# A decode kernel bound by its loads: softmax totals per pair of heads, three more folded value caches, other idle products, one value load cut 1 and 3

## The chip, the core and the metric

The kernel runs on one core of a Trainium2 chip, in one launch. A core has five engines that run apart from each other and meet at semaphores: TensorE (PE, matrix products; PEld is its weight load), VectorE (DVE), ScalarE (ACT), GpSimd (POOL) and SyncE (SP), which here only issues loads. Loads from HBM into on-chip memory (SBUF, 128 partitions) are carried out by 16 DMA engines. Products land in a second, small memory (PSUM). The metric is the device time of one execution in microseconds (us); lower is better.

## The reference

Two layers of attention for one new token over long key and value caches, each followed by a gated MLP, and each run twice with the same weights and caches:

```python
def _A_ref(x, k_cache, v_cache, wq, wo):
    B, Sq, D = x.shape
    H, Dh = 32, 128
    q = (lambda x, *d: x.transpose(*d))((x @ wq).reshape(B, Sq, H, Dh), 0, 2, 1, 3)
    scores = jnp.einsum("bhqd,bhkd->bhqk", q, k_cache) * (Dh ** -0.5)
    p = _softmax(scores, axis=-1)
    o = jnp.einsum("bhqk,bhkd->bhqd", p, v_cache)
    return (lambda x, *d: x.transpose(*d))(o, 0, 2, 1, 3).reshape(B, Sq, H * Dh) @ wo

x = x + _A_ref(_layernorm(x, axis=-1), A_k_cache, A_v_cache, A_wq, A_wo)
x = x + _B_ref(_layernorm(x, axis=-1), B_w_gate, B_w_up, B_w_down)
x = x + _A_ref(_layernorm(x, axis=-1), A_k_cache, A_v_cache, A_wq, A_wo)
x = x + _B_ref(_layernorm(x, axis=-1), B_w_gate, B_w_up, B_w_down)
```

B is 2, D is 576, the caches are [2, 32, 8192, 128] in float32 (268 MB each) and DF is 4608. Each attention reads both caches once, but for what the second finds still on chip from the first.

## The kernel before

**Items.** The caches are cut into 34 items, numbered 0 to 33. Items 0 to 29 (PAIRS is 30) are two neighbouring heads of one batch row: 8 MB of keys and 8 MB of values each, held as 128 partitions of 16384 numbers, 64 partitions a head. Even items are batch row 0 and odd ones row 1 of the same heads, so items 2j and 2j+1 belong together. Items 30 to 33 are single heads (SINGLE), 4 MB each. An item has 8 parts (4 for a single head) of 16 cache rows (PART, 2048 numbers a partition). Attention 0 goes through the items upwards, attention 1 downwards. Below, "keys 29" is the key cache of item 29.

**One item.** `multiply` forms key times query on DVE (line 744) in three stretches of 3, 3 and 2 parts; POOL adds the halves of each row (line 773); `add_up` sums the rest on DVE (line 776) and gives the stretch of SBUF free. Then `peak`, `highest` and `softmax` find the maximum and the weights, `total` (line 841) sums the weights over the partitions with a product with ones, `inverse` (line 847) takes the reciprocal on DVE, and `values` (line 909) multiplies weights and values on PE. An item's last `add_up` stands after the start of the next item; `values` of an item stands in the middle of the next item.

**Folding.** For items where `folds(n)` is true, the last two parts of the values are not multiplied on PE: `weigh` scales them on DVE (line 876), POOL adds them up in three halvings (line 879), and `folded` takes the short rest to PE (line 887). The `weigh` and `folded` of item n stand in item n+2. Until then the values stay in SBUF, whereas unfolded values are free once `values` has run in item n+1.

**Where loads go.** SBUF holds six slots of 4 MB (SLOT), and a ring of four small places for weights. A list of loads is written down once (`plan_first`, `plan_mlp`, `plan_second`); a small model (`Arena`) walks through the program, and a load is issued on SP in the list's order as soon as its place is free in that model. SP then waits at run time for the instructions that freed the place, and everything behind a waiting load in SP's queue waits too. An item of two heads takes two neighbouring slots, of (0,1), (2,3) and (4,5) the pair that has been free for longest:

```python
for s in sorted(range(0, NSLOT, 2), key=lambda s: max(self.freed[s:s + 2])):
    at = self.slots(key, (s, s + 1), 8)
```

At the end of attention 0 the slots are named in the plan instead (the tuple or the last number):

```python
k(SINGLE[0], (0,))
half(("v", 0, last), vc, last, 0, 1)
half(("v", 0, last), vc, last, 4, 5)
k(SINGLE[1], (3,))
v(SINGLE[0], (4,))
```

So keys 30 go to slot 0, the first half of values 29 (`last`) to slot 1, the second half to slot 5, keys 31 to slot 3.

**Between the attentions.** Weights pass through the ring in pieces of about 1 MB, 4 places, while PE multiplies them. `idle_products` puts products whose result nobody reads between the pieces. Attention 1 starts with keys 33 to 31, or parts of them, still in SBUF; the rest of its first caches is loaded part by part into places as they come free (`plan_second`), the values of item 30 into the place of values 33.

Of the kernel before, what the change touches and what calls it, by code (L numbers as in the profile page):

```python
# [9 lines left out]
F32 = mybir.dt.float32  # L10
# [5 lines left out]
P = 128  # L16
# [3 lines left out]
DH = 128  # L20
# [7 lines left out]
GH = 4  # L28
# [97 lines left out]
def decode_layers(ctx, tc, x_in, kc, vc, wq, wo, wg, wu, wd, out):  # L126
    nc = tc.nc
    scale = DH ** -0.5

    consts = ctx.enter_context(tc.tile_pool(name="consts", bufs=1))  # L130
    work = ctx.enter_context(tc.tile_pool(name="work", bufs=2))
# [8 lines left out]
    for c in range(4):  # L140
        for s in range(2):
            lo = 32 * c + s * B
# [66 lines left out]
    def several_parts(key, src, n, k, m, where, first):  # L209

        def make():
            at = places[where][first:first + m]
            if not all(arena.clear(a, PART) for a in at):
                return False
            for i, a in enumerate(at):
                arena.take((key, k + i), a, PART)
                ready.setdefault(key, {})[k + i] = part(a)
            load(at[0], n, src, k, k + m)
            return True

        queue.append(make)
# [169 lines left out]
    def plan_second():  # L391

        for k in range(4):
            of_half(1, k)
        half_rows(("wq", 1, NU - 1), wq, single[-1], None)
        for k in range(4):
            of_half(0, k)
        last = PAIRS - 1
        k63, v63, k62, v62 = ("k", 1, SINGLE[3]), ("v", 1, SINGLE[3]), ("k", 1, SINGLE[2]), ("v", 1, SINGLE[2])

        for k in range(2):
            by_rows(("k", 1, SINGLE[1]), kc, SINGLE[1], k, True)
        first, pair = ("k", 1, SINGLE[0]), ("k", 1, last)
        one(first, kc, SINGLE[0], 0, None)
        by_rows(("k", 1, SINGLE[1]), kc, SINGLE[1], 2, False)
        several_parts(first, kc, SINGLE[0], 1, 2, k63, 0)
        one(first, kc, SINGLE[0], 3, (k63, 2))
        one(pair, kc, last, 0, (k63, 3))
        for k in range(0, 4, 2):
            several_parts(("v", 1, SINGLE[0]), vc, SINGLE[0], k, 2, v63, k)  # L410
        for k, m, where, at in ((1, 2, k62, 0), (3, 2, k62, 2), (5, 2, v62, 0), (7, 1, v62, 2)):
            several_parts(pair, kc, last, k, m, where, at)
        half(("k", 1, last - 1), kc, last - 1, 0, 5)
        half(("k", 1, last - 1), kc, last - 1, 4, 4)
# [77 lines left out]
        )  # L492

    spread()
    home = consts.tile([P, 3 * DH + 20], F32, name="home")

# [18 lines left out]
    smalls = [bank2[:, 4 * GH + P + 2 * i:4 * GH + P + 2 * i + 2] for i in range(2)]  # L515
    low = bank2[:, 4 * GH + P + 4:]
    share = low[:, :FOLD * JC]
    kept = psum1.tile([P, JC, DH], F32, name="kept")

# [17 lines left out]
    def small(p, n):  # L537

        if n > 2:
            return turned[0:p, 0:n]  # L540
        smalls.append(smalls.pop(0))
        return smalls[0][0:p, 0:n]


    def norm(split=False, then=None):
# [62 lines left out]
    def attention(layer):  # L608
# [12 lines left out]
        def half_products(h):  # L621

            for k in range(4):
                key = ("wq", 1, h, k)
                q_products(
                    ready.pop(key).rearrange("p (c w) -> p c w", w=EQ), 64 * k + 8 + 4 * h, h,
                    k == 0, h == 0 and k == 3,
                )
                done(key)
                if k > 0 if h else k < 3:  # L630
                    idle_products(1)

        if layer == 0:
            for us in GU[0]:
# [202 lines left out]
                )  # L837

        def total(n):
            tot[n] = small(P, 2)  # L840
            nc.tensor.matmul(tot[n][:, :ITEMS[n].heads], ones, rs.pop(n), start=True, stop=True)  # L841

        def inverse(n):
            it, t = ITEMS[n], tot.pop(n)
            if it.heads == 2:
                rinv[n] = work.tile([P, 2], F32, name="rinv", bufs=4)
                nc.vector.reciprocal(rinv[n], t)
            else:
                if it.h not in of_head:
                    of_head[it.h] = work.tile([P, 2], F32, name="rinv", bufs=4)  # L850
                rinv[n] = of_head[it.h]
                nc.vector.reciprocal(rinv[n][:, it.b:it.b + 1], t[:, 0:1])

        of_head = {}

# [6 lines left out]

        def folds(n):

            return 3 <= n < PAIRS - 3

        def weigh(n):

# [65 lines left out]
        def divide(n, by_scalar=False):  # L934
            it = ITEMS[n]
            lo = 32 * (it.h % GH)
            if it.heads == 1:
                r = rinv[n]
                nc.vector.tensor_tensor(
                    out=oT[lo:lo + 32, it.h // GH, :, :, :],  # L940
                    in0=po[lo:lo + 32, :, :2].unsqueeze(2).to_broadcast([32, GH, 2, B]),
                    in1=r[lo:lo + 32, :].unsqueeze(1).unsqueeze(1).to_broadcast([32, GH, 2, B]),
                    op=ALU.mult,
                )
                return
            for b, i in ((b, i) for b in range(B) for i in range(2)):
                to = oT[lo + 32 * i:lo + 32 * i + 32, it.h // GH, :, :, b]
                o = po[lo:lo + 32, :, 2 * b + i:2 * b + i + 1].to_broadcast([32, GH, 2])
                ri = rinv[n - it.b + b][lo:lo + 32, i:i + 1]
                if by_scalar:  # L950
                    nc.scalar.activation(to, o, AF.Copy, scale=ri)
                else:
                    nc.vector.tensor_tensor(out=to, in0=o, in1=ri.unsqueeze(1).to_broadcast([32, GH, 2]), op=ALU.mult)
# [147 lines left out]
    def mlp(layer):  # L1101
# [10 lines left out]
        def split_products(h):  # L1112

            steps = [(("g", layer, h, u), u, 0) for u in range(4)] + [(("gu", layer, h), 4, 0)]
            steps += [(("u", layer, h, u), u, 1) for u in range(4)]
            for key, u, g in steps:
                w = ready.pop(key).rearrange("p (k c w) -> p k c w", c=4, w=HG)
                for k in range(2):
                    for c in range(4):
                        nc.tensor.matmul(  # L1120
                            acc[32 * c:32 * c + 4 * B, h, :HG], window(u, 4 * k + 2 * g), w[:, k, c, :],
                            start=(key == steps[0][0] and k == 0), stop=(key == steps[-1][0] and k == 1),
                        )
# [102 lines left out]
```

## Time and profile before

| | |
|---|---|
| median of three runs | 2683.0 us (2681.78 to 2683.21) |
| profiled execution: its own time | 2682.85 us |
| its span, first to last instruction | 2681.1 us |
| DVE busy | 1989.8 us (74%) |
| POOL busy | 1551.8 us (58%) |
| PE busy | 909.0 us (34%) |
| ACT busy | 165.4 us (6%) |
| load queue (q1) | 1152.40 MB, 99.8% of 16 engines' span |

Times in the rows are in us from the span's start, unless marked ns. A row of the order of time has start, duration, engine and line, operation, written<-read with shapes, a count, and in brackets how long the engine idled before it and what ended that. A row of stretches has the length, then busy time and count of PE, PEld, DVE, ACT and POOL, the granted PE clock (1 is full speed), the DMA engines' busy share and GB/s. SPq rows are loads being issued; what the load then takes is not in that row. A row of the chain has start, duration and what the chain ran through.

### The profile page before, as it was taken

To read this page: it belongs to the slowest core of one execution; us is meant where nothing else is said; L and a number is where in the kernel's file an instruction comes from. 1 tells how busy PE (TensorE), PEld (TensorE's weight loads), DVE (VectorE), ACT (ScalarE), POOL (GpSimd) and SP (SyncE) were. 2 spreads that over 40 slices of the span, in tenths; PEclk is the share of its full clock that TensorE was granted. 3 is DMA by queue.
4 is the path that set the end of the run, shared out by engine and by line. 5 is a ranking of instruction groups with operands and counts; after the bars stand their busy time and mean duration, and the time that the engine had idled before them with its cause. 6 is when DMAs were issued, how large, how long until landed. Compare 5 with 4: busy or idle time off the path is not lost.

```text
span 2681.1 us, 15549 instructions
## 1 busy us (share of the span) xinstructions
PE 909.0 (34%) x6276; PEld 284.4 (11%) x6276; DVE 1989.8 (74%) x935; ACT 165.4 (6%) x792; POOL 1551.8 (58%) x407
## 2 busy tenths in 40 slices
PE   1323332233223223334663333223222323332346
PEld 0100000000000000111221100000000000000022
DVE  4878888888788878867037778888888888888740
ACT  0000000000000000001026000000000000000000
POOL 2546676667666766744028457666766666676520
PEclk8656655665566566566986665566566556655678
DMA  9999999999999999999999999999999999999998
GB/s 423 438 430 431 435 434 431 434 432 434 434 432 433 434 432 435 429 430 428 416 411 430 436 429 433 434 434 432 430 436 434 431 434 433 434 432 432 435 428 383
DMA packets 29352, 1153.40 MB, mean 430 GB/s; under 512 B 3272, under 2 KB 3296, under 8 KB 4320
## 3 DMA queue, kind: packets, MB, share of 16 engines
q1 hardware_dynamic: 29240, 1152.40, 99.8%
q8 instruction: 49, 0.80, 0.1%
q14 instruction: 23, 0.19, 0.0%
q10 hardware_dynamic: 40, 0.01, 0.0%
HBM read 1152.39 MB, written 0.00 MB: 430 GB/s over the span
## 4 chain that ended last, share of the span: by engine, by line
DMA 67%; DVE 19%; PE 8%; ACT 3%; POOL 2%; issue 1%; SPq 0%; another core or an unknown queue 0%; POOLq 0%; ACTq 0%; DVEq 0%
DMA space<-in_A_k_cache_dram 57%; DVE space L744 17%; PE acc L887 3%; DMA space<-in_A_v_cache_dram 3%; DMA space<-in_B_w_down_dram 2%; POOL space L773 2%; ACT prz L833 2%; DVE scores L776 2%; PE bank L659 1%; DMA space<-in_B_w_up_dram 1%; DMA space<-in_B_w_gate_dram 1%; PE bank L841 1%; PE bank L810 1%; DMA space<-in_A_wo_dram 1%; ACT space L766 0%
## 5 line engine op out<-in xcount | busy, mean ns | idle before, releaser
L773 POOL TENSOR_TENSOR space<-space 128x3072 f32<-128x3072 f32 (+4 forms) x221 | 1128.0, 5104 | 476.3 <-DVE space L744 331.3
L744 DVE TENSOR_TENSOR space<-space,bank 128x6144 f32<-128x6144 f32 (+4 forms) x223 | 1111.8, 4986 | 343.6 <-DMA space<-in_A_k_cache_dram 270.9
L909 PE MATMUL acc<-space,prz 128*16 128x512 f32 (+1 forms) x3328 | 520.0, 790 | 346.4 <-DMA space<-in_A_v_cache_dram 342.3
L776 DVE TENSOR_REDUCE scores<-space 128x48 f32<-128x3072 f32 (+4 forms) x223 | 569.0, 2551 | 90.8 <-POOL space L773 90.6
L879 POOL TENSOR_TENSOR space<-space 128x2048 f32<-128x2048 f32 x144 | 389.8, 2707 | 384.0 <-DVE space L876 360.7
L659 PE MATMUL bank<-qsb,few 4*64 4x128 f32 (+1 forms) x256 | 46.2, 437 | 889.9 <-DVE space L744 881.9
L876 DVE TENSOR_TENSOR space<-space,bank 128x4096 f32<-128x4096 f32 x48 | 212.2, 4420 | 1.8 <-DVE bank L871 0.2
L909 PEld LDWEIGHTS acc<-space,prz 128*16 128x16 f32 (+1 forms) x3328 | 106.4, 118 | 742.0 <-DMA space<-in_A_v_cache_dram 378.7
L825 ACT ACTIVATE nbs<-bank 128x2 f32<-128x2 f32 (+1 forms) x68 | 11.6, 171 | 2010.2 <-PE bank L810 1973.1
L659 PEld LDWEIGHTS bank<-qsb,few 4*64 4x64 f32 (+1 forms) x256 | 20.8, 202 | 909.9 <-DVE space L744 892.0
L581 POOL TENSOR_TENSOR rstd<-ve,few 128x1 f32<-128x1 f32 x4 | 2.2, 550 | 177.0 <-DVE ve L579 177.0
L887 PE MATMUL acc<-space,few 128*16 128x512 f32 x96 | 90.6, 1047 | 0.0
L802 PE MATMUL bank<-ident,m 128*1 128x128 f32 x68 | 20.3, 298 | 196.3 <-DVE m L800 196.1
L1147 DVE STREAM_TRANSPOSE gu<-acc 128x288 f32<-128x288 f32 x4 | 1.9, 483 | 93.4 <-ACT acc L1145 93.4
L841 PE MATMUL bank<-few 128*128 128x2 f32 x120 | 35.3, 363 | 81.4 <-ACT prz L833 81.4
L932 PE MATMUL bank<-few,wide 128*32 128x4 f32 (+1 forms) x272 | 21.8, 203 | 119.3 <-DVE wide L924 119.3
L833 ACT ACTIVATE prz<-scores,nbs 64x128 f32<-64x128 f32 (+1 forms) x128 | 50.7, 396 | 11.7 <-POOL prz L823 8.8
L766 ACT ACTIVATE space<-space 128x128 f32<-128x128 f32 x164 | 48.4, 296 | 19.8 <-DVE space L744 16.7
L810 PE MATMUL bank<-m,few 1*128 1x2 f32 (+1 forms) x136 | 38.5, 350 | 27.4 <-DVE m L808 27.4
L585 DVE TENSOR_TENSOR x<-bank,x 128x144 f32<-128x144 f32 x4 | 1.2, 308 | 59.1 <-PE bank L1183 39.3
L923 DVE TENSOR_TENSOR acc<-acc,few 128x512 f32<-128x512 f32 x34 | 23.1, 680 | 29.2 <-PE acc L909 29.2
L760 POOL TENSOR_TENSOR space<-space,qs 128x512 f32<-128x512 f32 x23 | 29.2, 1272 | 19.7 <-ACT qs L741 19.7
(103 smaller groups left out, 524.2 us busy)
## 6 DMA issues: line engine op xcount, KB each, us to landing
space<-in_A_k_cache_dram SPq DMA_DIRECT2D x6, 4096.0 KB
space<-in_A_v_cache_dram SPq DMA_DIRECT2D x5, 4096.0 KB
space<-in_B_w_gate_dram SPq DMA_DIRECT2D x8, 1152.0 KB
space<-in_B_w_up_dram SPq DMA_DIRECT2D x8, 1152.0 KB
space<-in_B_w_down_dram SPq DMA_DIRECT2D x8, 1152.0 KB
space<-in_A_wq_dram SPq DMA_DIRECT2D x9, 1024.0 KB
space<-in_A_wo_dram SPq DMA_DIRECT2D x2, 4608.0 KB
space<-in_A_v_cache_dram SPq DMA_DIRECT2D x4, 2048.0 KB
```

What stands on the lines that cost most here:

```text
L659: nc.tensor.matmul(qb[n][to, :], pick[32 * c:32 * c + 4, r:r + 1].to_broadcast([4, P // it.heads]), qsb[32 * c:32 * c + 4, (h % 4) * DH:(h ...
L744: nc.vector.tensor_tensor(out=u[:, :r, :], in0=t[:, :r, :], in1=qb[n].unsqueeze(1).to_broadcast([P, r, DH]), op=ALU.mult)
L766: nc.scalar.activation(u[:, j, :], u[:, j, :], AF.Copy, accum_out=S[n][:, base(n, k) + j:base(n, k) + j + 1])
L773: nc.gpsimd.tensor_tensor(out=half, in0=half, in1=u[:, :r, DH // 2:], op=ALU.add)
L776: nc.vector.tensor_reduce(out=S[n][:, base(n, k):base(n, k) + own_rows(n, k, m)], in_=prod.pop((n, k)), axis=AX.X, op=ALU.add)
L810: nc.tensor.matmul(mT[n][:, :heads], ones[0:1, :], m1[:, :heads], start=True, stop=True)
L833: nc.scalar.activation(pr[at, lo:].rearrange("p (g e) -> p g e", e=4)[:, 0:it.rows // 2 * it.heads:2 * it.heads, :], s[at, :it.rows].rearr ...
L841: nc.tensor.matmul(tot[n][:, :ITEMS[n].heads], ones, rs.pop(n), start=True, stop=True)
L876: nc.vector.tensor_tensor(out=t, in0=t, in1=share.unsqueeze(2).to_broadcast([P, rows, DH]), op=ALU.mult)
L879: nc.gpsimd.tensor_tensor(out=t[:, :rows - less], in0=t[:, :rows - less], in1=t[:, less:rows], op=ALU.add)
L887: nc.tensor.matmul(accumulator(n)[0:16, :], owner[:, 8 * ITEMS[n].b:8 * ITEMS[n].b + 16], part_at(arena.live[key, lo][0], 4 * DH), start=F ...
L909: nc.tensor.matmul(accumulator(n)[32 * c:32 * c + m, :], pr[:, at:at + m], t[g // 4][:, g % 4 * 4:g % 4 * 4 + 4, :].rearrange("p j d -> p ...
```

## The change

1. `folds(n)` becomes `layer < n < PAIRS - 3` in place of `3 <= n < PAIRS - 3`: items 1 and 2 of attention 0 and item 2 of attention 1 are folded too.
2. `total` makes one product of 4 columns for two items that belong together, once the second is through, in place of one of 2 columns for each; `inverse` takes one reciprocal of 4 columns. The small PSUM places are given out anew for it, and `home` is 2 columns longer.
3. `idle_products`: between the query weights of attention 1, one product of 512 columns into the idle half of `acc` in place of two of 128 into another bank; between the second half of the first MLP's weights, mostly one of 256 columns into `acc` in place of two of 128.
4. Values 30 for attention 1 are loaded as 1 and 3 parts in place of 2 and 2, and parts 5 to 7 of keys 29 as 1 and 2 in place of 2 and 1.

```diff
-        for k in range(0, 4, 2):
-            several_parts(("v", 1, SINGLE[0]), vc, SINGLE[0], k, 2, v63, k)
-        for k, m, where, at in ((1, 2, k62, 0), (3, 2, k62, 2), (5, 2, v62, 0), (7, 1, v62, 2)):
+        for k, m in ((0, 1), (1, 3)):
+            several_parts(("v", 1, SINGLE[0]), vc, SINGLE[0], k, m, v63, k)
+        for k, m, where, at in ((1, 2, k62, 0), (3, 2, k62, 2), (5, 1, v62, 0), (6, 2, v62, 1)):
             several_parts(pair, kc, last, k, m, where, at)
...
                 if k > 0 if h else k < 3:
-                    idle_products(1)
+                    idle_products(2, 1 - h)
...
         def total(n):
-            tot[n] = small(P, 2)
-            nc.tensor.matmul(tot[n][:, :ITEMS[n].heads], ones, rs.pop(n), start=True, stop=True)
+
+            if ITEMS[n].heads == 1:
+                tot[n] = four[:, 0:1]
+                nc.tensor.matmul(tot[n], ones, rs.pop(n), start=True, stop=True)
+            elif completes(seq.index(n)):
+                tot[n] = four
+                nc.tensor.matmul(tot[n], ones, sums.rearrange("p a i -> p (a i)"), start=True, stop=True)
 
         def inverse(n):
-            it, t = ITEMS[n], tot.pop(n)
-            if it.heads == 2:
-                rinv[n] = work.tile([P, 2], F32, name="rinv", bufs=4)
+            it, t = ITEMS[n], tot.pop(n, None)
+            if it.heads == 2 and t is not None:
+                rinv[n] = work.tile([P, 4], F32, name="rinv", bufs=3)
                 nc.vector.reciprocal(rinv[n], t)
...
         def folds(n):
 
-            return 3 <= n < PAIRS - 3
+            return layer < n < PAIRS - 3
...
-                ri = rinv[n - it.b + b][lo:lo + 32, i:i + 1]
+                ri = rinv[n][lo:lo + 32, 2 * b + i:2 * b + i + 1]
...
                 if key != steps[-1][0]:
-                    idle_products(1, None if h else 1)
+                    idle_products(1, 1 - h if h == 0 or u else None)
```

How the order moves, at three places. In these rows `_49` is the part of a semaphore's name that all share. DMAHW0 to DMAHW7 count landings: the loads take the eight in turn, so a row that waits for DMAHW3 waits for the landing of one certain earlier load. DVE, PE, Activation and Pool are those engines' counts of done work.

First, SP's queue at the end of attention 0. The first two rows are keys 29 and values 28; keys 28, values 27, keys 29 and values 28 signal DMAHW1, 2, 3 and 4. The rows of 128x8192 are keys 30, the two halves of values 29, keys 31, values 30 and keys 32:

```order
 L168 DMA space<-in_A_k_cache_dram 128x16384 [waits DMAHW0_49,DVE_49,PE_49]
 L168 DMA space<-in_A_v_cache_dram 128x16384 [waits DMAHW2_49,PE_49]
-L168 DMA space<-in_A_k_cache_dram 128x8192 [waits DMAHW1_49,DVE_49]
+L168 DMA space<-in_A_k_cache_dram 128x8192 [waits DMAHW3_49,DVE_49]
 L168 DMA space<-in_A_v_cache_dram 128x8192 [waits DVE_49]
-L168 DMA space<-in_A_v_cache_dram 128x8192 [waits DMAHW4_49,PE_49]
-L168 DMA space<-in_A_k_cache_dram 128x8192 [waits DMAHW3_49,DVE_49]
+L168 DMA space<-in_A_v_cache_dram 128x8192 [waits DMAHW1_49]
+L168 DMA space<-in_A_k_cache_dram 128x8192 [waits DMAHW4_49,PE_49]
 L168 DMA space<-in_A_v_cache_dram 128x8192
 L168 DMA space<-in_A_k_cache_dram 128x8192
```

The order of the loads is the same, but slots 0 and 1, into which keys 30 and half of values 29 go, hold other caches by then. The three pairs of slots go round; as two more items are folded early on, each later cache stands two steps further round. Followed through `pair`, from the first loads on:

| cache | slots before | slots now |
|---|---|---|
| values 1, keys 4 | (4,5), (0,1) | (4,5), (4,5) |
| values 2, keys 5 | (4,5), (2,3) | (0,1), (0,1) |
| keys 28 | (0,1) | (4,5) |
| values 27 | (4,5) | (2,3) |
| keys 29 | (2,3) | (0,1) |
| values 28 | (4,5) | (2,3) |

Before, keys 30 wait until DVE is done with the first parts of keys 28; now they wait for the landing of keys 29 and until DVE is done with the first four parts of keys 29 (the sum over its second stretch).

Second, SP's queue at the start of attention 1, values 30 and then parts 1 to 7 of keys 29:

```order
 L168 DMA space<-in_A_k_cache_dram 128x4096
 L168 DMA space<-in_A_k_cache_dram 128x2048 x2
-L168 DMA space<-in_A_v_cache_dram 128x4096 x2
-L168 DMA space<-in_A_k_cache_dram 128x4096 x3
+L168 DMA space<-in_A_v_cache_dram 128x2048
+L168 DMA space<-in_A_v_cache_dram 128x6144
+L168 DMA space<-in_A_k_cache_dram 128x4096 x2
 L168 DMA space<-in_A_k_cache_dram 128x2048
+L168 DMA space<-in_A_k_cache_dram 128x4096
```

The first load of values 30 is one part and needs one part of the place free; the second needs the other three.

Third, PE at the same start, between the products with the query weights (line 616 before, 615 now), before:

```order
L616 MATMUL acc<-space,xt 4x512 x8
L592 MATMUL bank_124<-ident 4x128 x2
L616 MATMUL acc<-space,xt 4x512 x4
L592 MATMUL bank_124<-ident 4x128 x2
L616 MATMUL acc<-space,xt 4x512 x4
```

and now:

```order
L615 MATMUL acc<-space,xt 4x512 x8
L591 MATMUL acc<-ident 4x512
L615 MATMUL acc<-space,xt 4x512 x4
L591 MATMUL acc<-ident 4x512
L615 MATMUL acc<-space,xt 4x512 x4
```

The idle product is twice as many columns in one, and goes to the half of `acc` that the products beside it do not write.

More of the change, by code (lines that the diff above doesn't have):

```diff
@@ L494, in decode_layers @@
     spread()
-    home = consts.tile([P, 3 * DH + 20], F32, name="home")
+    home = consts.tile([P, 3 * DH + 22], F32, name="home")
     xt = consts.tile([P, PAD + NU * 32], F32, name="xt")
@@ L514, in decode_layers @@
     turned = bank2[:, 4 * GH:4 * GH + P]
-    smalls = [bank2[:, 4 * GH + P + 2 * i:4 * GH + P + 2 * i + 2] for i in range(2)]
-    low = bank2[:, 4 * GH + P + 4:]
+    pair, four = bank2[:, 4 * GH + P:4 * GH + P + 2], bank2[:, 4 * GH + P + 2:4 * GH + P + 6]
+    low = bank2[:, 4 * GH + P + 6:]
     share = low[:, :FOLD * JC]
@@ L540, in small @@
             return turned[0:p, 0:n]
-        smalls.append(smalls.pop(0))
-        return smalls[0][0:p, 0:n]
+        return pair[0:p, 0:n]
     def norm(split=False, then=None):
@@ L839, in total @@
         def total(n):
-            tot[n] = small(P, 2)
-            nc.tensor.matmul(tot[n][:, :ITEMS[n].heads], ones, rs.pop(n), start=True, stop=True)
+            if ITEMS[n].heads == 1:
[4 more added lines that the diff above has]
+                nc.tensor.matmul(tot[n], ones, sums.rearrange("p a i -> p (a i)"), start=True, stop=True)
         def inverse(n):
-            it, t = ITEMS[n], tot.pop(n)
-            if it.heads == 2:
-                rinv[n] = work.tile([P, 2], F32, name="rinv", bufs=4)
+            it, t = ITEMS[n], tot.pop(n, None)
+            if it.heads == 2 and t is not None:
+                rinv[n] = work.tile([P, 4], F32, name="rinv", bufs=3)
                 nc.vector.reciprocal(rinv[n], t)
-            else:
+            elif it.heads == 1:
                 if it.h not in of_head:
-                    of_head[it.h] = work.tile([P, 2], F32, name="rinv", bufs=4)
-                rinv[n] = of_head[it.h]
-                nc.vector.reciprocal(rinv[n][:, it.b:it.b + 1], t[:, 0:1])
+                    of_head[it.h] = work.tile([P, 4], F32, name="rinv", bufs=3)
+                rinv[n] = of_head[it.h][:, 0:2]
+                nc.vector.reciprocal(rinv[n][:, it.b:it.b + 1], t)
         of_head = {}
```

## The prediction

> **What bounds the kernel now.** I read the page's totals first, then stretches, then the order of time where the stretches stand out.
>
> ```profile
> span 2681.1 us, 15549 instructions
> DMA  9999999999999999999999999999999999999998
> GB/s 423 438 430 431 435 434 431 434 432 434 434 432 433 434 432 435 429 430 428 416 411 430 436 429 433 434 434 432 430 436 434 431 434 433 434 432 432 435 428 383
> q1 hardware_dynamic: 29240, 1152.40, 99.8%
> ```
>
> The load queue q1 has packets on the engines for 99.8% of the span, and the slices' GB/s row stays between 411 and 438 but for the last. A kernel whose loads never pause is as long as its bytes at that rate, plus whatever time the DMA engines stand still. So for each edit I ask one thing: does it add or remove a pause of the loads?
>
> ```profile
> 0.00:10.00 10.00, 0.00 (x0) 0.00 (x0) 4.41 (x29) 0.00 (x0) 0.70 (x6) 1.00 0.85 340
> 1160.00:1170.00 10.00, 0.66 (x9) 0.56 (x8) 9.96 (x6) 1.04 (x4) 9.30 (x2) 0.50 0.90 387
> 1400.00:1410.00 10.00, 5.55 (x34) 1.26 (x34) 8.98 (x8) 7.55 (x50) 9.36 (x8) 0.83 0.96 375
> 2670.00:2680.00 10.00, 6.32 (x148) 3.68 (x146) 0.31 (x1) 0.00 (x0) 0.00 (x0) 1.00 0.46 184
> ```
>
> In these stretches the last two numbers are the DMA share and GB/s. Pauses before are few: some 2 us at the start (340 of 433 GB/s), the last microseconds, when all has landed, and 10 x (1 - 375/433) = 1.3 us at 1400. The 387 at 1160 is an effect of where 10 us are cut, as packets are counted whole: the 67 us slice it lies in (the 18th) runs at 430. Nothing in this kernel can then win more than a few us, and a gap of 5.4 us (0.2% of 2683, about what a measurement of this kernel can tell from no change) has to come from a new pause.
>
> **The folds, at the end of attention 0: the term that decides.** Loads of two-head items run one behind the other:
>
> ```profile
> 1084.84 27.13 DMA space<-in_A_k_cache_dram
> 1111.99 6.57 DVE space L744
> 1123.53 27.15 DMA space<-in_A_k_cache_dram
> 1150.70 6.56 DVE space L744
> ```
>
> These are links of the chain of waits. DVE starts keys 28 at 1111.99 and keys 29 at 1150.70, each as it lands; between them lie two loads of 8.39 MB, so one takes 19.35 us (433 GB/s) and one of half that size 9.7 us. Now SP and DVE before the change, where keys 29 are worked on:
>
> ```profile
> 1141.33 0.33 SPq L168 DMA_DIRECT2D space<-in_A_v_cache_dram  x1
> 1141.75 0.38 SPq L168 DMA_DIRECT2D space<-in_A_k_cache_dram  x1
> 1142.18 37.60 SPq L168 DMA_DIRECT2D space<-in_A_v_cache_dram  x2
> 1150.70 6.55 DVE L744 TENSOR_TENSOR space<-space,bank 128x6144 f32<-128x6144 f32 x1 [9.82 <-DMA space<-in_A_k_cache_dram]
> 1170.07 9.31 PE L909 MATMUL acc<-space,prz 128*16 128x512 f32 x64 [3.28 <-DMA space<-in_A_v_cache_dram]
> 1173.60 3.35 DVE L776 TENSOR_REDUCE scores<-space 128x48 f32<-128x3072 f32 x1
> 1178.43 2.29 DVE L776 TENSOR_REDUCE scores<-space 128x32 f32<-128x2048 f32 x1 [1.49 <-POOL space L773]
> 1180.75 0.33 SPq L168 DMA_DIRECT2D space<-in_A_k_cache_dram  x1
> ```
>
> SP issues values 28 at 1141.33, keys 30 at 1141.75 and the first half of values 29 at 1142.18 (that row merges it with the second half, at the end of its 37.60 us). Keys 30 thus stand in the queue 28 us before values 28 land (1170.07, where PE starts on them), and follow without a gap: they land near 1170.07 + 9.7 = 1179.8.
>
> Now slot 0 holds keys 29 when keys 30 are due. Keys 30 need its four parts, three of the first stretch and one of the second, so they wait for DVE's second sum over 48 rows: it starts at 1173.60 and ends at 1173.60 + 3.35 = 1176.95. Nothing in the change moves that sum: keys 29 still land at 1150.7, and DVE works through without a break that could be closed. Everything behind keys 30 in SP's queue waits too, and all that was issued ahead of them has landed by 1170.07. So the loads run dry. Keys 30 then land at 1176.95 + 9.7 plus what a load costs from issue to landing beyond its bytes when nothing runs ahead of it. The trace shows that for the output's 2 KB:
>
> ```profile
> 2678.02 0.65 SPq L1198 DMA_DIRECT2D out_dram<-x  x1
> ...
> SPq L1222 <- DMA out_dram<-x: 1.3, 1, 1.3
> ```
>
> 0.65 + 1.3 = 1.95 us. Keys 30 land at 1188.6 in place of 1179.8: 8.8 us later. Ends of this term: with no such cost 6.9 us; with the loss of the stretch at 1400, where the queue also ran nearly dry, on top of the 1.95 (a slow restart) 10.2 us. I take 8.8, as the output's row is a load path measured alone.
>
> Is there a second pause behind it? The half of values 29 waits for the last sum of keys 29, which ends at 1178.43 + 2.29 = 1180.7; keys 30 keep the engines busy until past 1187, so that is covered. The second half, freed early now, and keys 31, which wait for PE's 9.31 us on values 28 (to 1179.4), follow at once. Is the delay made up later? Compute behind it is fed by these loads and shifts with them; only pauses that exist before could shrink, and the 1.3 us at 1400 is the one in the way. So the delay stays.
>
> **The folds elsewhere.** Each new fold costs what a fold costs:
>
> ```profile
> L879 POOL TENSOR_TENSOR space<-space 128x2048 f32<-128x2048 f32 x144 | 389.8, 2707 | 384.0 <-DVE space L876 360.7
> L876 DVE TENSOR_TENSOR space<-space,bank 128x4096 f32<-128x4096 f32 x48 | 212.2, 4420 | 1.8 <-DVE bank L871 0.2
> L887 PE MATMUL acc<-space,few 128*16 128x512 f32 x96 | 90.6, 1047 | 0.0
> ```
>
> 4.4 us of DVE, 3 x 2.7 = 8.1 us of POOL, and 8 product groups fewer on PE. Early in attention 0, DVE runs dry waiting for keys in every round, so the time itself is covered. What moves is the release: keys 4 now wait for the fold of values 1, as all keys from 6 on already do.
>
> ```profile
> 142.41 6.57 DVE space L744
> 297.47 6.57 DVE space L744
> 309.01 27.14 DMA space<-in_A_k_cache_dram
> ```
>
> DVE starts keys 7 at 297.47, and the next keys are issued 11.5 us after that, at 309.01; values issued ahead keep the engines busy for 19.35 us, so 7.8 us are to spare. Keys 3 are started at 142.41, keys 4 now issued near 154.0, due by 161.8: no pause. Keys 5 likewise. If that cover were gone, the loads would pause by the overshoot.
>
> At the end of attention 1, values 0 now wait for the fold of values 2:
>
> ```profile
> 2529.24 2.29 DVE L776 TENSOR_REDUCE scores<-space 128x32 f32<-128x2048 f32 x1 [1.48 <-POOL space L773]
> 2531.43 0.80 SPq L168 DMA_DIRECT2D space<-in_A_v_cache_dram  x2
> 2541.64 2.29 DVE L744 TENSOR_TENSOR space<-space,bank 128x2048 f32<-128x2048 f32 x1 [9.79 <-DMA space<-in_A_k_cache_dram]
> ```
>
> The last sum of keys 1 ends at 2531.5, then 4.4 us DVE (idle there until 2541.64), 8.1 us POOL, 1 to 2 us PE: values 0 issued near 2546, in place of 2531.8. Keys 0 land at 2541.6 and values 1 19.35 us later, at 2561. 15 us to spare: nothing. The following weight loads get other places and wait for other readers, all of them due before the queue is dry.
>
> **Totals once per pair.**
>
> ```profile
> L841 PE MATMUL bank<-few x120: 352/362/374, 82.6 to 2575.3; 128*128 128x2 f32 x120
> L847 DVE RECIPROCAL rinv<-bank x60: 160/163/170, 87.3 to 2575.7; 128x2 f32<-128x2 f32 x60
> ```
>
> About 30 items with one PE product and one reciprocal less: 30 x 2 x 0.36 and 30 x 0.16 us, on engines that wait for loads in every round. Worth nothing here; if a round were compute-bound it would be some 0.2 us each.
>
> **Idle products and the load cut 1 and 3.** Both act at the start of attention 1.
>
> ```profile
> 1368.22 1.02 PE L592 MATMUL acc<-ident 128*4 128x512 f32 x2
> 1372.26 0.60 PE L592 MATMUL bank<-ident 128*4 128x128 f32 x4
> 1374.87 1.04 PE L616 MATMUL acc<-space,xt 128*4 128x512 f32 x8 [2.01 <-DMA space<-in_A_wq_dram]
> 1377.37 1.89 PE L616 MATMUL acc<-space,xt 128*4 128x512 f32 x8 [0.89 <-DMA space<-in_A_wq_dram]
> ...
> 1370.00:1380.00 10.00, 6.73 (x48) 1.79 (x52) 0.15 (x2) 0.00 (x0) 0.55 (x1) 0.80 1.01 412
> ...
> 1400.04 5.24 PE L909 MATMUL acc<-space,prz 128*8 128x512 f32 x32 [0.82 <-ACT qs L741]
> 1403.63 2.04 SPq L168 DMA_DIRECT2D space<-in_A_v_cache_dram  x2
> ```
>
> Lines 616 are query products, 592 idle ones. After 1.02 and 0.60 us fillers PE still idles up to 2.01 us between pieces of weights, and at 1377.37 the same eight products take 1.89 us in place of 1.04: the granted clock has halved (0.80 over the stretch). With 1.02 us fillers throughout, the 2.0 us gap shrinks to 1.6. If that keeps the clock, the last query products end 1.89 - 1.04 = 0.9 us earlier, and so does the work on keys 33 and all that releases places behind it. The first load of values 30 waits for PE's values 33 (1400.04, 5.24 us for four parts): 2 parts before, issued at 1403.63; now 1 part, some 1.3 us earlier. Together they close the pause of 1.3 us at 1400. Without the clock, the cut alone closes it there, but the same late compute chain holds up the next loads and the gain is mostly given back. Ends: -1.3 and 0; a fatter filler that delays a piece could cost some tenths, which the pieces in flight cover. I take -1.0, near the full gain: the drop comes right behind the 2.01 us gap, and both edits work on the same pause.
>
> The Trainium skill, in "TensorE: Matmul & The Clock Gate" (Part 1), puts the clock at half only after at least one idle window of about 3.4 us. Here it fell after gaps of no more than 2.01 us, so the trace does not agree, unless idle shares and not whole windows count. By the page neither filler would matter: the gain would be 0 and the time the one of the second case below.
>
> In the first MLP, 4 products of 128 columns become 2 of 256: 0.60 us either way by the 592 rows of equal width. Nothing.
>
> **Sum.** +8.8 - 1.0 = +7.8 us on the profiled execution: span 2681.1 to 2688.9, its time 2682.85 to 2690.7. The median of the three runs stands 0.15 us above that execution, so 2690.8 us.
>
> **Rivals.**
> - *The clock falls all the same.* For it: the remaining gap of 1.6 us. Then +8.8: 2691.8.
> - *Not slower: keys 30 do not wait.* If slot 0's keys were done by 1168, before values 28 land, there would be no pause, and only the gain is left: 2682.0. It decides at the end of that sum: 1176.95 less 1170.07 is 6.9 us late, so DVE's part on keys 29 (26 us in a row) would have to be a quarter shorter. Nothing in the rows offers that; what remains is that I followed the slots wrongly.
> - *Another new wait runs dry too.* Early folds if the fold comes over 7.8 us late, values 0 if over 15 us. One overshoot of some us gives about 2695. Against it: those margins, and rounds that repeat within 0.3 us.
> - *Clearly faster* would need no pause and more than 5.4 us won, more than all pauses in the way.
>
> **Numbers.** Forecast 0.53, clock falls 0.30, no pause 0.07, another pause 0.06, everything else 0.04. Ends of the two terms together: 6.9 - 1.3 = +5.6 gives 2688.6, 10.2 + 0 gives 2693.2; I add 0.6 us below and 0.3 above for runs that differ by 1.4 us: 2688.0 to 2693.5. Slower by over 0.2% (above 2688.4): 0.90; within 0.2%: 0.08; faster: 0.02. The first two cases and the other pause lie above the line but for their lowest sizes.
>
> **What would show it.** Right: no loads between about 1170 and 1178, SP's row for keys 30 near 1177 with DVE's sum as what it waited for, and all that follows 7 to 10 us late; keys 4 near 154 and values 0 near 2546 without a drop of GB/s; products at 1377 (shifted) at 1.04 us and no dip at 1400. Wrong: keys 30 issued near 1141, or a dip at 160 or 2561.

## The result

The changed kernel takes 2691.96 us (median of 6 runs, 2691.47 to 2692.9), the kernel before beside it 2682.62 us (6 runs, 2681.64 to 2683.56). The ratio is 1.0035, with a 95% interval of 1.0022 to 1.0048: 9.3 us slower, where 7.8 were forecast. The profiled execution of the changed kernel has a span of 2690.1 us, 9.0 more than before. All lines of the code stand 1 to 4 numbers away from those before: 743 is the multiplication of the keys, 775 the sum, 913 the values, 615 a query product, 591 an idle product.

The same rows of the page as before:

```profile
span 2690.1 us, 15325 instructions
GB/s 421 436 435 434 431 432 434 434 434 433 433 432 433 432 433 435 434 360 426 422 417 424 437 435 435 433 429 435 432 434 436 431 432 434 435 432 431 435 428 383
q1 hardware_dynamic: 29240, 1152.40, 99.4%
```

The bytes are the same. The 18th slice fell from 430 to 360 GB/s: over its 67 us that is 67 x (1 - 360/430) = 11 us of loads not carried. No other slice moved by more than 6 GB/s. The stretches around it, with those around 1400 us (length, busy time and count of PE, PEld, DVE, ACT and POOL, PE clock, DMA share, GB/s):

```profile
1160.00:1170.00 10.00, 0.61 (x8) 0.57 (x9) 9.97 (x5) 1.04 (x4) 9.32 (x2) 0.50 0.64 275
1170.00:1180.00 10.00, 8.77 (x64) 2.11 (x64) 8.50 (x3) 0.00 (x0) 5.91 (x2) 0.82 0.28 93
1180.00:1190.00 10.00, 0.27 (x1) 0.08 (x1) 1.74 (x3) 0.00 (x0) 0.00 (x0) 0.69 1.01 433
1410.00:1420.00 10.00, 4.82 (x34) 1.11 (x26) 8.43 (x8) 8.14 (x54) 9.48 (x8) 0.84 1.03 432
1460.00:1470.00 10.00, 1.04 (x8) 0.00 (x0) 9.82 (x9) 8.96 (x59) 10.00 (x8) 0.67 0.92 371
```

And the order of time on SP, DVE and PE at the pause:

```profile
1150.56 6.55 DVE L743 TENSOR_TENSOR space<-space,bank 128x6144 f32<-128x6144 f32 x1 [9.80 <-DMA space<-in_A_k_cache_dram]
1170.02 8.77 PE L913 MATMUL acc<-space,prz 128*16 128x512 f32 x64 [3.37 <-DMA space<-in_A_v_cache_dram]
1173.39 3.35 DVE L775 TENSOR_REDUCE scores<-space 128x48 f32<-128x3072 f32 x1
1176.77 0.33 SPq L168 DMA_DIRECT2D space<-in_A_k_cache_dram  x1
1180.56 0.82 SPq L168 DMA_DIRECT2D space<-in_A_v_cache_dram  x2
1189.07 2.29 DVE L743 TENSOR_TENSOR space<-space,bank 128x2048 f32<-128x2048 f32 x1 [8.22 <-DMA space<-in_A_k_cache_dram]
```

Keys 30 are issued at 1176.77, 0.03 us after DVE's second sum over keys 29 ends (1173.39 + 3.35); before, at 1141.75. Values 28 landed at 1170.02, and nothing was queued behind them. The dip of 1400 us (375 GB/s before) is gone at its place 9 us later (432); another one, of 371, stands at 1460, where the kernel before carried 440 (1450 to 1460). The folds elsewhere show as forecast: keys 4 are issued at 152.00, and the second load in the row of values 1 and values 0 ends being issued at 2540.32 + 16.38 = 2556.7, with no drop of GB/s at either place:

```profile
152.00 0.33 SPq L168 DMA_DIRECT2D space<-in_A_k_cache_dram  x1
2540.32 16.38 SPq L168 DMA_DIRECT2D space<-in_A_v_cache_dram  x2
...
150.00:160.00 10.00, 2.59 (x11) 0.75 (x11) 9.97 (x4) 2.19 (x9) 9.35 (x2) 0.50 1.06 459
160.00:170.00 10.00, 7.69 (x48) 1.73 (x48) 8.59 (x4) 0.00 (x0) 7.57 (x2) 0.67 1.04 447
2560.00:2570.00 10.00, 0.72 (x12) 0.70 (x16) 9.90 (x12) 0.00 (x0) 5.59 (x3) 0.50 0.98 426
```

### The profile page after: what moved, and what is told of

Read it like the earlier page. It is cut to its first block, busy times and chain, and to the rows that moved or that the text cites. A ratio compares the mean times of both kernels' runs of the same rounds, so it can differ in the third digit from the quotient of the medians.

```text
span 2690.1 us, 15325 instructions
## 1 busy us (share of the span) xinstructions
PE 885.2 (33%) x6150; PEld 268.4 (10%) x6150; DVE 2001.8 (74%) x911; ACT 165.7 (6%) x792; POOL 1576.8 (59%) x416
## 4 chain that ended last, share of the span: by engine, by line
DMA 65%; DVE 21%; PE 8%; POOL 3%; ACT 2%; issue 2%; another core or an unknown queue 0%; SPq 0%; POOLq 0%; ACTq 0%; DVEq 0%
DMA space<-in_A_k_cache_dram 58%; DVE space L743 18%; PE acc L891 3%; DMA space<-in_B_w_down_dram 3%; DMA space<-in_B_w_gate_dram 2%; DVE scores L775 2%; POOL space L772 2%; PE bank L658 1%; DMA space<-in_B_w_up_dram 1%; PE bank L809 1%; ACT prz L832 1%; DMA space<-in_A_wo_dram 1%; PE bank L845 1%; ACT space L765 0%; PE acc L913 0%
## 5 line engine op out<-in xcount | busy, mean ns | idle before, releaser
L883 POOL TENSOR_TENSOR space<-space 128x2048 f32<-128x2048 f32 x153 | 414.4, 2708 | 408.7 <-DVE space L880 392.8
L913 PE MATMUL acc<-space,prz 128*16 128x512 f32 (+1 forms) x3280 | 506.3, 782 | 351.9 <-DMA space<-in_A_v_cache_dram 343.8
L880 DVE TENSOR_TENSOR space<-space,bank 128x4096 f32<-128x4096 f32 x51 | 225.4, 4421 | 2.0 <-DVE bank L875 0.3
L891 PE MATMUL acc<-space,few 128*16 128x512 f32 x102 | 96.4, 1049 | 0.9 <-POOL space L883 0.9
L936 PEld LDWEIGHTS bank<-few,wide 128*32 128x32 f32 x272 | 19.1, 154 | 216.2 <-issue 211.1
L955 ACT ACTIVATE oT<-bank,rinv 32x8 f32<-32x8 f32 x108 | 28.1, 260 | 190.1 <-PE bank L936 189.1
```

What stands on the lines that cost most here:

```text
L880: nc.vector.tensor_tensor(out=t, in0=t, in1=share.unsqueeze(2).to_broadcast([P, rows, DH]), op=ALU.mult)
L883: nc.gpsimd.tensor_tensor(out=t[:, :rows - less], in0=t[:, :rows - less], in1=t[:, less:rows], op=ALU.add)
L891: nc.tensor.matmul(accumulator(n)[0:16, :], owner[:, 8 * ITEMS[n].b:8 * ITEMS[n].b + 16], part_at(arena.live[key, lo][0], 4 * DH), start=F ...
L913: nc.tensor.matmul(accumulator(n)[32 * c:32 * c + m, :], pr[:, at:at + m], t[g // 4][:, g % 4 * 4:g % 4 * 4 + 4, :].rearrange("p j d -> p ...
L936: nc.tensor.matmul(po[lo:lo + 32, i, :c], t[:, i::GH], of[:, :c], start=True, stop=True)
```

## The experiments

Four explanations were held against each other. Theory A: the slots; the new folds move keys 29 into the place that keys 30 are due in. Theory B: each fold costs by its work, wherever it stands. Theory C: one of the other edits costs the time. Theory D: the time hangs on when DVE gets keys 30, and not on the loads standing still. The kernel before ran beside each group; its medians were 2683.0 us (first four experiments), 2682.8 (the next three) and 2682.95 (the last two), so a time is read against these. Where a standing time of the DMA engines is given, it is added up over the packets of the run's trace: the time in which an engine has none, averaged over the 16.

### The old folds, everything else changed

```diff
-            return layer < n < PAIRS - 3
+            return 3 <= n < PAIRS - 3
```

> The changed kernel with folded values only from item 3 on, as before; totals, idle products and the cut 1 and 3 stay. Theory A (slots: the two items more that are folded in attention 0 put keys 29 where keys 30 are due, and the loads pause about 9 us there): the pause is gone, keys 30 are issued near 1141 us again, and the time is that of the kernel before within 1 us (2682 to 2683; the changed one 2692). Theory B (work: each fold more costs about 3 us wherever it stands): also that of before. Theory C (one of the other edits costs the 9 us): it stays at 2692. So this run tells C from A and B.

Measured: 2682.66 us (11 runs), ratio 1.0000 (0.9991 to 1.0009). The 18th slice is back, and keys 30 are issued early:

```profile
span 2680.3 us, 15389 instructions
GB/s 423 437 436 427 435 434 432 433 433 435 434 433 433 433 432 435 431 428 429 419 415 438 428 435 434 434 433 430 435 432 433 434 434 430 437 432 430 438 426 376
...
1139.61 0.38 SPq L168 DMA_DIRECT2D space<-in_A_k_cache_dram  x1
```

Theory C falls: the whole of it comes with the folds.

### One cache fewer folded in attention 0

```diff
-            return layer < n < PAIRS - 3
+            return 2 <= n < PAIRS - 3
```

> The changed kernel with values folded from item 2 on in both layers: one cache more than before in each attention, two in all in place of three. Theory A: the slots rotate by one step, keys 29 sit in slots 4 and 5, keys 30 wait for keys 28 only and are issued near 1141 us: no pause, 2682 to 2683, as before. Theory B: two folds at 3 us each, 2688 to 2689.

Measured: 2682.74 us (11 runs), ratio 0.9999 (0.9990 to 1.0008).

```profile
span 2680.9 us, 15349 instructions
...
1140.48 0.38 SPq L168 DMA_DIRECT2D space<-in_A_k_cache_dram  x1
```

Two of the three new folds cost nothing that can be measured. Theory B falls: at some 3 us each it asked for 2688 to 2689. It is also the direct test of two statements of the prediction, that the fold of item 2 in attention 1 is free and that a fold in attention 0 is free in itself.

### Three more folded in attention 0

```diff
-            return layer < n < PAIRS - 3
+            return 2 * layer <= n < PAIRS - 3
```

> The changed kernel with three items more folded in attention 0 (0, 1 and 2; attention 1 as in the changed kernel): four caches more than before. In the order of loads keys 29 still sit in slots 0 and 1. Theory A: the same pause of about 9 us and no more, 2691 to 2693. Theory B: four folds at 3 us, 2694 to 2696.

Measured: 2693.98 us (5 runs), ratio 1.0042 (1.0029 to 1.0054), 11.0 us above the kernel before, where the changed kernel stood 9.3 above. The pause at keys 30 is the same: the engines stand 10.1 us around it in both. Part of the surplus is a second, small pause that the theory's number had left out, at 100 us:

```profile
101.70 0.33 SPq L168 DMA_DIRECT2D space<-in_A_v_cache_dram  x1
1178.35 0.33 SPq L168 DMA_DIRECT2D space<-in_A_k_cache_dram  x1
...
100.00:110.00 10.00, 0.37 (x1) 0.08 (x1) 9.39 (x5) 0.00 (x0) 2.69 (x1) 0.50 0.82 322
```

With item 0 folded too, values 1 can't take the slots of values 0 and go where keys 1 were; they wait for the last sum over keys 1 (99.38 + 2.29 = 101.67 on DVE) and are issued at 101.70. In the changed kernel they were issued at 92.82, and this stretch carried 420 GB/s. 10 x (1 - 322/420) = 2.3 us by the stretch, in which packets are counted whole; the engines stand 1.1 us there, and the difference of the times is 1.7 us, so some tenths stay open. By its time alone this run lies outside A's range and 0.02 us below B's; the rows, and the run before, speak for A: it is the mechanism of theory A at a second place.

### The four parts that keys 30 overwrite first

```diff
+            if layer == 0 and n == PAIRS - 1:
+                return [(0, 4), (4, 2), (6, 2)]
             return [(0, 3), (3, 3), (6, 2)]
```

> The changed kernel, but DVE multiplies keys 29 in stretches of 4, 2 and 2 parts in place of 3, 3 and 2, so that the first sum already frees all four parts that keys 30 overwrite. From the rows of the changed kernel: POOL's halving of four parts ends near 1168.3 (1150.6 + 8.7 + 4/3 x 6.7), the sum over 64 rows 4.45 us later, near 1172.8 instead of 1176.7. Theory A: keys 30 are issued 4 us earlier, the pause shrinks by as much, and the time is 4 us less, 2688. Theories B and C: no change, 2692.

Measured: 2689.27 us (9 runs), ratio 1.0024 (1.0015 to 1.0034): 6.3 us above the kernel before in place of 9.3, so 3.0 less, where 4 were expected. B and C expected none.

```profile
1172.52 0.33 SPq L168 DMA_DIRECT2D space<-in_A_k_cache_dram  x1
1183.84 0.80 SPq L168 DMA_DIRECT2D space<-in_A_v_cache_dram  x2
1184.85 2.29 DVE L745 TENSOR_TENSOR space<-space,bank 128x2048 f32<-128x2048 f32 x1 [0.72 <-DMA space<-in_A_k_cache_dram]
...
1180.00:1190.00 10.00, 1.75 (x7) 1.27 (x7) 7.03 (x5) 1.15 (x5) 3.84 (x2) 0.70 0.91 367
```

Keys 30 come 4.25 us earlier (1172.52 for 1176.77) and are in use 4.2 us earlier (1184.85 for 1189.07). But the half of values 29 behind them still waits for the last sum over keys 29, and this sum now ends later, at 1183.8. By then keys 30 have all but landed: the loads thin out a second time (367 GB/s in a stretch that carried 433), and some of the gain goes there. The time follows the pause of the loads, with the size of both pauses together: the engines stand 6.9 us in all, where the changed kernel has 10.1, and the 3.2 us between them match the 3.0 us of the times.

### The half of values 29 ahead of keys 30

```diff
-        k(SINGLE[0], (0,))
-        half(("v", 0, last), vc, last, 0, 1)
         half(("v", 0, last), vc, last, 4, 5)
+        k(SINGLE[0], (0,))
+        half(("v", 0, last), vc, last, 0, 1)
```

> The changed kernel with all three folds, but with one step of the order of loads moved: the second half of values 29 (slot 5, free since keys 28) stands ahead of keys 30 in the queue, not behind. Theory A: keys 30 are still issued near 1176.7 us, when DVE's second sum over keys 29 ends, but the half issued near 1141 keeps the engines busy from 1170.1 to 1179.8, so the loads do not pause: 2681.5 to 2683.5. Keys 30 land as late as in the changed kernel (near 1189), so if what counts is when DVE gets keys 30 and not whether the loads stand still (theory D), the time stays near 2692.

Measured: 2683.04 us (11 runs), ratio 1.0001 (0.9992 to 1.0010). All three folds are in.

```profile
1139.75 0.98 SPq L168 DMA_DIRECT2D space<-in_A_v_cache_dram  x2
1176.71 0.33 SPq L168 DMA_DIRECT2D space<-in_A_k_cache_dram  x1
1190.08 2.29 DVE L743 TENSOR_TENSOR space<-space,bank 128x2048 f32<-128x2048 f32 x1 [9.30 <-DMA space<-in_A_k_cache_dram]
...
1170.00:1180.00 10.00, 9.56 (x64) 2.17 (x64) 8.51 (x3) 0.00 (x0) 5.83 (x2) 0.74 0.93 382
```

Keys 30 are issued as late as in the changed kernel (1176.71) and reach DVE later still (1190.08 for 1189.07), and it costs nothing that the times can show, because another 4 MB stood in the queue meanwhile: 382 GB/s where the changed kernel carried 93, and 0.8 us of standing engines in place of 10.1. Theory D falls, and theory B with it, as the work of all three folds is still there. One line of the list of loads takes the whole loss away.

### The other edits one by one

The idle products alone, on the kernel before:

```diff
-                    idle_products(1)
+                    idle_products(2, 1 - h)
...
-                    idle_products(1, None if h else 1)
+                    idle_products(1, 1 - h if h == 0 or u else None)
```

> The kernel before with the wider idle products alone. By my forecast: the granted clock stays up at the query products of attention 1 (all at 1.04 us up to the last, none at 1.89), and a part of the pause at 1400 us, 0.7 us of standing DMA engines before, goes: 0 to 0.7 us, which the times cannot show. Rival: the clock falls at 1376 as before (a product row of 1.89 us near 1377), and nothing changes.

The cut of the loads alone, on the kernel before:

```diff
-        for k in range(0, 4, 2):
-            several_parts(("v", 1, SINGLE[0]), vc, SINGLE[0], k, 2, v63, k)
+        for k, m in ((0, 1), (1, 3)):
+            several_parts(("v", 1, SINGLE[0]), vc, SINGLE[0], k, m, v63, k)
-        for k, m, where, at in ((1, 2, k62, 0), (3, 2, k62, 2), (5, 2, v62, 0), (7, 1, v62, 2)):
+        for k, m, where, at in ((1, 2, k62, 0), (3, 2, k62, 2), (5, 1, v62, 0), (6, 2, v62, 1)):
```

> The kernel before with the loads of values 30 cut 1 and 3 alone (and the next key parts 1 and 2 with it). By my forecast: the first load of values 30 is issued some 1.3 us earlier (1402.3 for 1403.6), the dip at 1400 us closes or nearly, and what follows is held up as before, because the query products still run at the halved clock: 0 to 0.7 us, which the times cannot show. Rival: the pause only moves behind it, to 1410 to 1460, at the same size.

The totals alone, on the kernel before (the edits of `total`, `inverse` and `divide` shown with the change):

> The kernel before with the totals once per pair of heads alone. By my forecast nothing: within 1 us of the kernel before, with the pause of 0.7 us at 1400 us still there. Rival: the reciprocals of 4 columns behind the pair's second item are late for the division of its result and cost some tenths in each of 30 pairs, 2685 or more.

The folds alone, on the kernel before:

```diff
-            return 3 <= n < PAIRS - 3
+            return layer < n < PAIRS - 3
```

> The kernel before with the three folds more alone. By theory A the pause at keys 30 is there (loads standing from about 1169 to 1178 us) and nothing makes up for it. The changed kernel lies 9.7 us above the same kernel with the old folds (2691.96 against 2682.66, less 0.4 us by which the kernel before stood higher beside the second), and 0.6 us of standing engines near 1400 us is there as before: 9 to 10.5 us slower, 2692 to 2693. If the pause and the other edits hang together in some other way, this differs from that sum.

| alone, on the kernel before | us (runs) | ratio, 95% interval |
|---|---|---|
| idle products | 2682.57 (8) | 1.0000 (0.9989 to 1.0010) |
| cut 1 and 3 | 2682.80 (8) | 1.0001 (0.9991 to 1.0011) |
| totals per pair | 2682.23 (10) | 0.9997 (0.9988 to 1.0006) |
| three more folds | 2692.83 (5) | 1.0036 (1.0022 to 1.0051) |

The folds alone give 9.9 us, as the sum asked. The totals cost nothing, and the rival's 2685 is ruled out. For the other two the profiles say more than the times. First, where 1400 us dips, in the kernel with the idle products, with the cut, with the folds alone (in this last one 9 us later) and with the totals alone:

```profile
1400.00:1410.00 10.00, 5.87 (x34) 1.23 (x26) 8.80 (x8) 7.76 (x51) 9.48 (x8) 0.67 1.00 417
```

```profile
1401.60 3.70 SPq L168 DMA_DIRECT2D space<-in_A_v_cache_dram  x2
...
1400.00:1410.00 10.00, 5.22 (x34) 1.11 (x26) 8.68 (x8) 7.90 (x52) 9.49 (x8) 0.84 1.03 430
1450.00:1460.00 10.00, 1.58 (x12) 0.15 (x4) 9.82 (x9) 8.97 (x58) 10.00 (x9) 0.67 0.93 378
```

```profile
1410.00:1420.00 10.00, 6.17 (x34) 1.29 (x26) 8.49 (x8) 8.07 (x53) 9.49 (x8) 0.67 1.01 424
1460.00:1470.00 10.00, 0.69 (x8) 0.00 (x0) 9.82 (x9) 8.97 (x59) 10.00 (x9) 0.64 0.98 397
```

```profile
1400.00:1410.00 10.00, 5.20 (x34) 1.13 (x26) 8.63 (x8) 7.93 (x53) 9.49 (x8) 0.84 1.00 410
```

With the cut alone the first load of values 30 is issued at 1401.60, 2.0 us earlier than before (1.3 expected), and the dip only moves, to 1450 (378), as the rival of that run had it. With the idle products there is none to speak of. But with the folds alone, which have the old idle products and the old cut, it is gone from its place too, with a shallow one at 1460 (397). With the totals alone, where it was expected to stay, 410 stands at 1400 and 399 at 1420. So the dip is no fixed price that these edits remove: its place and depth differ between executions that share the idle products and the cut. Second, the query products on which the clock was read, with the idle products alone, the old folds, the totals alone and the folds alone:

```profile
1377.44 1.04 PE L616 MATMUL acc<-space,xt 128*4 128x512 f32 x8 [2.07 <-DMA space<-in_A_wq_dram]
1379.93 1.04 PE L616 MATMUL acc<-space,xt 128*4 128x512 f32 x8 [0.61 <-DMA space<-in_A_wq_dram]
```

```profile
1379.66 1.04 PE L615 MATMUL acc<-space,xt 128*4 128x512 f32 x8 [1.72 <-DMA space<-in_A_wq_dram]
1382.24 1.59 PE L615 MATMUL acc<-space,xt 128*4 128x512 f32 x8 [0.17 <-DMA space<-in_A_wq_dram]
1384.62 2.05 PE L615 MATMUL acc<-space,xt 128*4 128x512 f32 x8
```

```profile
1377.33 1.04 PE L615 MATMUL acc<-space,xt 128*4 128x512 f32 x8 [2.23 <-DMA space<-in_A_wq_dram]
1382.39 1.81 PE L615 MATMUL acc<-space,xt 128*4 128x512 f32 x8 [0.16 <-DMA space<-in_A_wq_dram]
```

```profile
1384.70 1.04 PE L616 MATMUL acc<-space,xt 128*4 128x512 f32 x8 [1.02 <-DMA space<-in_A_wq_dram]
1397.07 1.04 PE L616 MATMUL acc<-space,xt 128*4 128x512 f32 x8 [1.03 <-DMA space<-in_A_wq_dram]
```

With wide fillers the clock stayed up past a gap of 2.07 us once, and fell after one of 1.72 us another time. With narrow ones it fell after 2.23 us, and stayed up through all products where the gaps were 1.0 us. Over all eleven profiles, the clock fell during the query products in three of the seven with wide fillers and in three of the four with narrow ones. So neither the filler nor the longest gap alone decides it; where the one long gap falls differs from one execution to the next.

None of the nine kernels beats the kernel before. Six of them, among them the one with all three folds and the moved load, are level with it and beat the changed kernel by 9 us.

## Why the prediction was right, and where it was not

**The deciding term, right.** Keys 30 wait for DVE's second sum (1176.74; forecast 1176.95), nothing covers the time from 1170 on, and nothing gives the delay back. Taking the folds back, turning the slots by another number of steps, freeing the parts earlier and putting another load ahead each moved the time as this chain asks, and the folds alone bring it all.

**Its size, somewhat small.** 8.8 us were forecast. Here keys 30 are in use 12.30 us after they are issued (1189.07 - 1176.77); less 9.7 us for the bytes, a load into an empty queue costs 2.6 us, not the 1.95 us taken from the output, which is a write of 2 KB and no load. That makes 1176.77 - 1170.02 + 2.6 = 9.3 us. The folds alone measured 9.9 us, and the changed kernel's span is 9.8 us above that with the old folds (2690.1 - 2680.3); the rest is within what the runs differ by. All lie inside the ends given, 6.9 to 10.2.

**The folds elsewhere, right.** Keys 4 at 152.00 (forecast 154.0), values 0 at some 2556 (2546 plus the delay of 9), no pause at either. The margin is real and not wide: the run that folds item 0 as well runs dry for a moment, only not for the reason given (a late fold) but for the one of the deciding term (a slot whose reader is later).

**Totals and MLP fillers, right:** nothing that the times can show (2682.23 us with the totals alone; the MLP fillers were run only together with the other idle products, 2682.57).

**Idle products and cut, -1.0 us: the step that failed.** The signs that it named were there in the changed kernel: products at 1.04 us where 1.89 stood, no dip at 1400. That was luck, not the mechanism: the clock fell all the same, only later, at the sixth group of query products, and a dip of like size stands at 1460 (371 GB/s):

```profile
1389.56 1.04 PE L615 MATMUL acc<-space,xt 128*4 128x512 f32 x8 [0.60 <-DMA space<-in_A_wq_dram]
1392.13 1.89 PE L615 MATMUL acc<-space,xt 128*4 128x512 f32 x8 [0.18 <-DMA space<-in_A_wq_dram]
```

The path was wrong. A clock that stays up was to end the last query products 0.9 us earlier, and with them the work behind. But the last group waits for its weights at either clock. Its row before, where several groups ahead of it are slow, and with the idle products alone, where none is:

```profile
1389.76 1.04 PE L616 MATMUL acc<-space,xt 128*4 128x512 f32 x8 [0.79 <-DMA space<-in_A_wq_dram]
```

```profile
1389.86 1.04 PE L616 MATMUL acc<-space,xt 128*4 128x512 f32 x8 [0.63 <-DMA space<-in_A_wq_dram]
```

PE's products with values 33 then start at 1400.04 and 1399.78, and the first load of values 30 is issued at 1403.63 and 1403.43: 0.2 us, not 0.9.

The size was wrong too: 1.3 us was read off one stretch of 10 us, in which packets are counted whole. In the kernel before the engines stand 0.5 us there (1395 to 1420), and 0.8 us from 1380 to 1500. In that longer stretch they stand 0.7 us with the totals alone, 0.8 with the cut alone, 0.3 with the idle products alone and 0.2 with the old folds; 9 us later, it is 0.7 us in the changed kernel and 0.3 with the folds alone, which have neither edit. So without the pause at keys 30 the profiles with wide idle products have some 0.5 us less of it, in the run with the old folds although the clock fell; behind the pause it is the other way round. What decides it stays open. Against the 9.9 us of the folds alone, all other edits together are worth 9.9 - 9.3 = 0.6 us, and against the kernel before -0.3 us in the run with the old folds: no gain that these runs could tell from none. The measured time, 2691.96, is therefore next to that of the rival in which the clock falls all the same (2691.8). The 1.5 us between 7.8 and 9.3 are both errors together: the 1.0 us that did not come, and 0.5 us that the deciding term was short.

The Trainium skill, in "TensorE: Matmul & The Clock Gate" (Part 1), has the clock at half after at least one idle window of about 3.4 us, in windows that run freely and do not start with the kernel. No gap between the query products reached 3.4 us (the longest, with the cut alone, was 2.36 us), and the clock fell in six of the eleven profiles, so the traces go on disagreeing with the idle window taken whole; that the same products keep the clock in one execution and lose it in another would fit windows that are not tied to the kernel, which is an argument and not a test. No run here shows the windows themselves, and what decides the clock stays open.

## What to carry to other kernels

Where loads rotate through places, an edit that changes how long one buffer is held changes which place every later load gets, also far from the edit. So follow the places to the next spot where they are written down by hand, and ask there who frees the place and when the queue runs dry. If it does, look first for another load that could stand ahead of the waiting one: here that was worth 9 us without touching the compute. And a dip of a microsecond in a single stretch is no price yet: see first whether what it is blamed on ends last. Here the slow products were done in time for the last weights.

## What the runs showed of the hardware

A load into an empty queue took 2.4 to 2.8 us more than its bytes: from its issue to DVE's start on it, 12.30 us in the changed kernel, 12.33 with the four parts first (1184.85 - 1172.52), 12.13 with three items folded early in attention 0 (DVE starts on keys 30 at 1190.48, after 1178.35), 12.47 with the folds alone (1189.33 - 1176.86), each for 4 MB that take 9.7 us in a full queue. The Trainium skill, in "DMA: Bandwidth & Descriptors" (Anatomy of one DMA), states a fixed cost of some 2.0 us for a transfer issued from GpSimd; these loads are issued from SP, and took 0.4 to 0.8 us more than that.

And a pause begins before the last load has landed. The stretches of 1 us of the kernel before, and then of the changed one:

```profile
1167.00:1168.00 1.00, 0.00 (x0) 0.00 (x0) 1.00 (x1) 0.87 (x4) 1.00 (x1) 0.50 0.68 295
1168.00:1169.00 1.00, 0.00 (x0) 0.00 (x0) 1.00 (x1) 0.00 (x0) 1.00 (x1) 0.50 0.76 328
```

```profile
1167.00:1168.00 1.00, 0.00 (x0) 0.00 (x0) 1.00 (x1) 0.74 (x3) 1.00 (x1) 0.50 0.15 66
1168.00:1169.00 1.00, 0.00 (x0) 0.00 (x0) 1.00 (x1) 0.00 (x0) 1.00 (x1) 0.50 0.00 0
```

A packet is counted where it begins. Before, engines that were through with their share of values 28 began on the next load from 1167 on; in the changed kernel no packet of values 28 begins after 1168, and the last are still under way: by the packets of its trace, the first of the 16 engines is through at 1166.0 and the last at 1169.4, and PE starts on values 28 at 1170.02. The engines end a load at different times, and a load queued behind it hides that; an empty queue lays it bare. The first packet of keys 30 begins at 1177.7, 1.0 us after their issue. So to cost nothing at all, a load would have to be issued some 5 us before the one ahead of it has landed, not just by then (an estimate from these numbers, 1170.0 - 1166.0 + 1.0; no run tests it).
